# Two half-width matmuls side by side for a last block of 64, a reordered start, and paired row blocks in a two-product SiLU kernel

## The chip, the cores and the metric

One core of a Trainium2 chip. The metric is the device time of one execution in microseconds (us); lower is better.

## The reference, cut to what matters

```python
B, S, D, F = 1, 2048, 640, 1728          # bfloat16
h   = jax.nn.silu(jnp.einsum("bsd,df->bsf", x, w1))
out = jnp.einsum("bsf,fd->bsd", h, w2)
```

The number to notice is F = 1728 = 13 x 128 + 64. The kernel hands the tensor engine blocks of 128 rows by 128 columns (`128*128` in the profile lines below), so F gives 13 full blocks and one block of 64.

## The kernel before

x is transposed to `xT_sb`: chunk 0 (512 rows) on the tensor engine against an identity matrix, the other three chunks by transposing DMAs. The first product computes h transposed, in units of one f-block by 512 rows: five matmuls of 512 columns, one for each 128 rows of D. The matmuls write their sums to `ps1` and `ps2`, the kernel's two tensors in the memory called PSUM. The scalar engine computes the sigmoid from PSUM and the vector engine multiplies it with PSUM into `hT_sb`. The second product runs over 16 row blocks `st` of 128 rows. For each of the FT = 14 f-blocks it issues one matmul of 512 output columns and one of 128 (`DA` and `DB`, together D = 640).

The last f-block is padded with zeros from 64 to 128 and treated like the others:

```python
FT = (F + P - 1) // P                     # 14
N_WARM_MM = 11
...
for i, (sc, ft, c0, n) in enumerate(units):          # first product, ft runs over all 14
    ...
    for dt in range(DT):
        ins = pe.matmul(ps1[:, buf, 0:n],
            lhsT=w1_sb[:, dt, ft * P:(ft + 1) * P],
            rhs=xT_sb[:, dt, col0:col0 + n], start=(dt == 0), stop=(dt == DT - 1))
    ins.then_inc(sem_pe1, 1)
    if i == TP_INSERT_AFTER:                          # 0: after the very first unit
        for j in range(hj, JB):                       # x blocks 2 and 3
            transpose_block(j)
...
for ft in range(FT):                                  # second product
    for (st, ci, b2, c0, ncol) in seg:
        ins = pe.matmul(ps2[:, b2, c0:c0 + ncol],
            lhsT=hT_sb[:, ft, st * P:(st + 1) * P],
            rhs=w2_sb[:, ft, d0:d0 + ncol], start=(ft == 0), stop=(ft == FT - 1))
```

The first two f-blocks of chunk 0 are split into "half-units" of 256 rows, so that work can start when half of this chunk is transposed. Before that, 11 warm-up matmuls on zeros run while x is loaded.

## Time and profile before

The time was 133.96 us (median of 4) when the prediction was made.

| part of the profiled execution (132.13 us) | length |
|---|---|
| head: start to the end of the half-units | 10.26 us |
| first product, 512-column units | 58.27 us |
| second product | 61.02 us |
| end of the last matmul to the end of the span | 2.58 us |

The span runs from the first to the last instruction of the profiled execution; device times are about 1.8 us longer. The borders are starts of matmuls read from the trace; where such a record is missing, as that of the first 512-column matmul here, its start is taken from its neighbours. The last border is the end of the last matmul, and ends of matmuls are modelled by the profiler.

From the page of the kernel before, first the busy time of each engine, then the chain of work that ended last (followed back from the last instruction, at each step to what released it), as shares of the span by engine and by line:

```profile
PE 126.5 (96%) x755; PEld 65.4 (49%) x769; DVE 52.0 (39%) x78; ACT 40.5 (31%) x79; POOL 1.9 (1%) x10
PE 95%; DVE 2%; issue 1%; ACT 0%; POOL 0%; DVEq 0%; POOLq 0%
PE ps L335 46%; PE ps L295 45%; PE ps L246 3%; DVE xT_sb L414 2%; PE ps L260 0%; ACT o_sb L396 0%; POOL z_sb L159 0%; DVEq L413 0%; POOLq L464 0%
```

Line 295 is the first product, line 335 the second, line 246 the warm-up, line 260 the transposes. The chain is tensor engine nearly from end to end. The busy share alone would not say so, because the recorded times of successive matmuls overlap. The groups, kept apart by shape, show this (count, busy us, mean ns of one):

```profile
L335 PE MATMUL ps<-w_sb,hT_sb 128*128 128x512 bf16 x216 | 58.1, 379 | 0.0
L295 PE MATMUL ps<-xT_sb,w_sb 128*128 128x512 bf16 x264 | 58.0, 379 | 0.3
L335 PE MATMUL ps<-w_sb,hT_sb 128*128 128x128 bf16 x224 | 44.6, 219 | 0.4
```

A 512-column matmul is recorded at 379 ns, but its successor starts 216 ns after it; for 128 columns it is 219 ns and 56 ns. What a matmul costs in a dense stream is the distance between starts. The next answer of the profile gives the busy time of each engine in three stretches: 512-column units of the first product, second product, tail.

```profile
core 0: us, PE busy (x) PEld busy (x) DVE busy (x) ACT busy (x) POOL busy (x), PEclk, DMA share, GB/s
10.26:68.53 58.27, 57.95 (x266) 26.41 (x270) 37.07 (x55) 32.07 (x55) 0.00 (x0) 1.00 0.34 79
68.53:129.55 61.02, 60.60 (x441) 34.41 (x447) 12.05 (x17) 4.33 (x15) 0.00 (x0) 1.00 0.11 39
```

The tensor engine fills both stretches; vector and scalar engine have time to spare. (Some matmul records are missing from a trace: there are 270 weight loads but 266 matmuls in the first line.)

The head, as the tensor engine's own timeline (start, length of the merged run, line, shape, count, and the idle time before it with what ended it):

```profile
1.10 4.46 PE L246 MATMUL ps<-z_sb 128*128 128x512 bf16 x11 [1.10 <-POOL z_sb L159]
5.40 0.72 PE L260 MATMUL ps<-ident,x_sb 128*128 128x128 bf16 x10
7.04 0.72 PE L295 MATMUL ps<-xT_sb,w_sb 128*128 128x256 bf16 x5 [0.91 <-DVE xT_sb L414]
7.59 0.72 PE L260 MATMUL ps<-ident,x_sb 128*128 128x128 bf16 x10
8.15 0.71 PE L295 MATMUL ps<-xT_sb,w_sb 128*128 128x256 bf16 x5
9.15 1.27 PE L295 MATMUL ps<-xT_sb,w_sb 128*128 128x256 bf16 x10 [0.29 <-DVE xT_sb L414]
```

Twice the tensor engine stands still, for 0.91 and 0.29 us, until the vector engine's casts (copies with a change of type) of the transposed x are done (line 414).

### The profile page before, as it was taken

How to read it: one execution, taken by the hardware profiler on the slowest of the kernel's cores; microseconds unless marked ns; L12 is line 12 of the kernel's file. 1: busy time of each engine (PE TensorE's matmuls, PEld its weight loads, DVE VectorE, ACT ScalarE, POOL GpSimd, SP SyncE). 2: the span in 40 equal slices, each digit the busy share in tenths (PEclk: the TensorE clock that was granted, in tenths of full speed). 3: DMA queues.
4: the chain of work that ended last, by engine and by line, in shares of the span. 5: the costliest groups of instructions: out<-in, count | busy, mean ns of one | idle time of the engine just before them, and what ended most of it. 6: DMA issues, size and time to landing. Idle time of an engine off the chain costs nothing.

```text
span 132.1 us, 1876 instructions
## 1 busy us (share of the span) xinstructions
PE 126.5 (96%) x755; PEld 65.4 (49%) x769; DVE 52.0 (39%) x78; ACT 40.5 (31%) x79; POOL 1.9 (1%) x10
## 2 busy tenths in 40 slices
PE   6879999999999999999999999999999999999992
PEld 2365444444444444444445555555555555555461
DVE  0164666666666666666662122222102222220121
ACT  4235555555555555555550000000000000000001
POOL 5000000000000000000000000000000000000000
DMA  3897474599800000000000111101111110011103
GB/s 102 249 371 213 100 76 111 100 369 289 159 2 0 5 0 2 0 0 0 0 0 5 50 50 50 40 15 50 50 50 50 54 50 19 31 50 55 50 0 99
DMA packets 15672, 9.78 MB, mean 74 GB/s; under 512 B 8816, under 2 KB 15664, under 8 KB 15664
## 3 DMA queue, kind: packets, MB, share of 16 engines
q1 hardware_dynamic: 14464, 8.95, 25.0%
q10 hardware_dynamic: 1200, 0.72, 1.8%
q8 instruction: 6, 0.10, 0.3%
q14 instruction: 2, 0.02, 0.0%
HBM read 5.08 MB, written 2.62 MB: 58 GB/s over the span
## 4 chain that ended last, share of the span: by engine, by line
PE 95%; DVE 2%; issue 1%; ACT 0%; POOL 0%; DVEq 0%; POOLq 0%
PE ps L335 46%; PE ps L295 45%; PE ps L246 3%; DVE xT_sb L414 2%; PE ps L260 0%; ACT o_sb L396 0%; POOL z_sb L159 0%; DVEq L413 0%; POOLq L464 0%
## 5 line engine op out<-in xcount | busy, mean ns | idle before, releaser
L295 PE MATMUL ps<-xT_sb,w_sb 128*128 128x512 bf16 (+1 forms) x284 | 60.7, 372 | 1.5 <-DVE xT_sb L414 1.2
L335 PE MATMUL ps<-w_sb,hT_sb 128*128 128x512 bf16 (+1 forms) x440 | 60.6, 298 | 0.4
L335 PEld LDWEIGHTS ps<-w_sb,hT_sb 128*128 128x128 bf16 x448 | 34.5, 98 | 26.7
L422 DVE TENSOR_TENSOR hT_sb<-ps,sig_sb 128x512 bf16<-128x512 f32 (+1 forms) x58 | 39.0, 673 | 22.0 <-ACT sig_sb L372 21.9
L295 PEld LDWEIGHTS ps<-xT_sb,w_sb 128*128 128x128 bf16 x290 | 28.2, 98 | 33.5 <-DVE xT_sb L414 1.7
L372 ACT ACTIVATE sig_sb<-ps 128x512 bf16<-128x512 f32 (+1 forms) x58 | 33.7, 583 | 27.0 <-PE ps L295 27.0
L435 DVE CAST o_sb<-ps 128x512 bf16<-128x512 f32 x14 | 9.7, 692 | 42.9 <-PE ps L335 42.9
L384 ACT CAST o_sb<-ps 128x128 bf16<-128x128 f32 x14 | 3.7, 266 | 49.2 <-PE ps L335 49.2
L246 PE MATMUL ps<-z_sb 128*128 128x512 bf16 x11 | 4.5, 590 | 1.1 <-POOL z_sb L159 1.1
L414 DVE CAST xT_sb<-ps 128x384 bf16<-128x384 f32 x4 | 2.0, 553 | 6.1 <-PE ps L260 6.1
L447 DVE CAST o_sb<-ps 128x1024 bf16<-128x1024 f32 x1 | 1.2, 1225 | 5.4 <-PE ps L335 5.4
L246 PEld LDWEIGHTS ps<-z_sb 128*128 128x128 bf16 x11 | 1.5, 144 | 3.6 <-issue 2.5
L396 ACT CAST o_sb<-ps 128x256 bf16<-128x256 f32 x1 | 0.4, 373 | 7.3 <-PE ps L335 7.3
L363 ACT CAST xT_sb<-ps 128x256 bf16<-128x256 f32 x4 | 1.3, 373 | 4.1 <-PE ps L260 4.1
L357 ACT ACT_TABLE_LOAD x1 | 1.3, 1283 | 1.8 <-issue 1.8
L260 PE MATMUL ps<-ident,x_sb 128*128 128x128 bf16 x20 | 1.4, 219 | 0.0
L260 PEld LDWEIGHTS ps<-ident,x_sb 128*128 128x128 bf16 x20 | 1.3, 98 | 0.3
L175 POOL MEMSET w_sb<- 128x640 bf16 x1 | 0.6, 633 | 0.0
L409 DVE MEMSET z_sb<- 128x128 uint32 x1 | 0.2, 165 | 0.8 <-PEq L464 0.8
L172 POOL MEMSET w_sb<- 128x320 bf16 x1 | 0.4, 366 | 0.0
L159 POOL MEMSET z_sb<- 128x256 bf16 x1 | 0.3, 313 | 0.3 <-POOLq L464 0.3
L162 POOL TENSOR_SCALAR_AFFINE_SELECT ident<-ident 128x128 bf16<-128x128 bf16 x1 | 0.3, 294 | 0.2 <-POOL ident L160 0.2
(7 smaller groups left out, 1.0 us busy)
## 6 DMA issues: line engine op xcount, KB each, us to landing
out_dram<-o_sb SPq DMA_DIRECT2D x14, 160.0 KB, 1.8
w_sb<-in_w_dram SPq DMA_DIRECT2D x1, 1120.0 KB, 8.9
w_sb<-in_w_dram SPq DMA_DIRECT2D x1, 960.0 KB, 6.2
w_sb<-in_w_dram SPq DMA_DIRECT2D x1, 880.0 KB, 6.7
w_sb<-in_w_dram SPq DMA_DIRECT2D x1, 640.0 KB, 5.0
x_sb<-in_x_dram SPq DMA_DIRECT2D x1, 320.0 KB, 3.7
x_sb<-in_x_dram ACTq DMA_DIRECT2D x1, 320.0 KB, 4.1
w_sb<-in_w_dram ACTq DMA_DIRECT2D x1, 320.0 KB, 4.6
```

Source lines behind the costliest of these rows:

```text
L246: pe.matmul(ps1[:, NB1 - 1, :], lhsT=z_sb[:, 0:P], rhs=z_sb[:, :], start=True, stop=True,)
L260: ins = pe.matmul(tp_views[wv][:, sl, :], lhsT=x0_sb[:, j, dt * P:(dt + 1) * P], rhs=ident[:, :], start=True, stop=True,)
L295: ins = pe.matmul(ps1[:, buf, 0:n], lhsT=w1_sb[:, dt, ft * P:(ft + 1) * P], rhs=xT_sb[:, dt, col0:col0 + n], start=(dt == 0), stop=(dt == ...
L335: ins = pe.matmul(ps2[:, b2, c0:c0 + ncol], lhsT=hT_sb[:, ft, st * P:(st + 1) * P], rhs=w2_sb[:, ft, d0:d0 + ncol], start=(ft == 0), stop= ...
L357: act.activation(out=warm_sb[:, :], in_=warm_sb[:, :], func=ACT.Sigmoid)
L363: act.copy(out=xT_sb[:, TPV:DT, j * P:(j + 1) * P], in_=tp_views[wv][:, s0_:s0_ + (DT - TPV), :],).then_inc(sem_tpc_a, 1)
L372: act.activation(out=sig_sb[:, buf, 0:n], in_=ps1[:, buf, 0:n], func=ACT.Sigmoid,).then_inc(sem_act1, 1)
L384: act.copy(out=o_sb[:, ob, DA:D], in_=ps2[:, b2, c0:c0 + ncol]).then_inc(sem_ev_a, 1)
L414: dve.tensor_copy(out=xT_sb[:, 0:TPV, j * P:(j + 1) * P], in_=tp_views[wv][:, s0_:s0_ + TPV, :],).then_inc(sem_tpc_v, 1)
L422: dve.tensor_tensor(out=hT_sb[:, ft, col0:col0 + n], in0=ps1[:, buf, 0:n], in1=sig_sb[:, buf, 0:n], op=ALU.mult,).then_inc(sem_dve1, 1)
L435: dve.tensor_copy(out=o_sb[:, ob, 0:DA], in_=ps2[:, b2, c0:c0 + ncol]).then_inc(sem_ev_v, 1)
L447: dve.tensor_copy(out=o_sb[:, obA:obA + 2, 0:DA], in_=ps2[:, bA_, 0:2 * DA].rearrange("p (t c) -> p t c", t=2),).then_inc(sem_ev_v, 1)
```

## The change

The intent is to stop paying a full block for the block of 64. The array is used as two halves. In the first product, the 64 columns of w1 are loaded into column half 0 for one chunk and column half 1 for another, and the two matmuls write PSUM partitions 0 to 63 and 64 to 127. In the second product the 64 rows of h's last block lie in partitions 0 to 63 for even chunks and 64 to 127 for odd ones, so a row block of an even and one of an odd chunk form a pair and use the two row halves. The second product is reordered into eight such pairs, which use `ps1` and `ps2` in turn. The short matmuls ("tail") come last in even pairs and first in odd ones, so that two tails are always neighbours.

With it come a new head (9 warm-up matmuls, all transposes before the first unit) and a new end (the last row block's 512-column part is finished and copied out under its 128-column part). The diff, cut to its core:

```diff
-    N_WARM_MM = 11
+    N_WARM_MM = 9
+            if sc == 3 and ft == 3:
+                units.append((-1, 0, 1, 0))        # tails of chunks 0 and 1
+                units.append((-1, 2, 3, 0))        # tails of chunks 2 and 3
...
-            hj = JB // 2
-            for j in range(hj):
+            for j in range(JB):
                 transpose_block(j)
...
+                    for dt in range(DT):
+                        for hh, scc in enumerate(chs):
+                            ins = pe.matmul(
+                                ps1[hh * 64:hh * 64 + F_LAST, buf, :],
+                                lhsT=w1_sb[:, dt, f0:f0 + F_LAST],
+                                rhs=xT_sb[:, dt, scc * SCH:(scc + 1) * SCH], ...)
...
+                tail_first = p % 2 == 1
+                def tail():
+                    for d0, ncol in ((0, DA), (DA, DB)):
+                        for h, st in enumerate(pr):
+                            ins = pe.matmul(
+                                view[:, h, d0:d0 + ncol],
+                                lhsT=hT_sb[64 * h:64 * h + 64, FT - 1, st * P:(st + 1) * P],
+                                rhs=w2_sb[64 * h:64 * h + 64, FT - 1, d0:d0 + ncol],
+                                start=tail_first, stop=not tail_first, ...)
+                def full(h, st, cols):
+                    for ft in range(FT - 1):
+                        for d0, ncol in cols:
+                            ins = pe.matmul(view[:, h, d0:d0 + ncol], ...)
+                if tail_first:
+                    tail()
+                for h, st in enumerate(pr):
+                    if p == NPAIR - 1 and h == 1:
+                        full(h, st, [(0, DA)])
+                        full(h, st, [(DA, DB)])
+                    else:
+                        full(h, st, [(0, DA), (DA, DB)])
+                if not tail_first:
+                    tail()
```

Cut: memsets, the second copy of w2's last block, semaphore counts, the copies out.

More of the change, by code (lines that the diff above doesn't have):

```diff
@@ L55, in bass_standalone__dense_activation_silu__prompt_kernel, with unit_chunks, tail_half @@
         units.append((0, ft, 0, HN))
-    TP_INSERT_AFTER = 0
     for ft in range(N_SPLIT_FT):
         units.append((0, ft, HN, HN))
-    for ft in range(N_SPLIT_FT, FT):
+    PACK_TAIL = (F_LAST <= 64) and (FT >= 2)
+    FT_REG = FT - 1 if PACK_TAIL else FT
+    for ft in range(N_SPLIT_FT, FT_REG):
         units.append((0, ft, 0, SCH))
     for sc in range(1, NSC):
-        for ft in range(FT):
+        for ft in range(FT_REG):
             units.append((sc, ft, 0, SCH))
-    NU = len(units)
-    chunk_done_cnt = {}
-    for i, (sc, ft, c0, n) in enumerate(units):
-        chunk_done_cnt[sc] = i + 1
+            if sc == 3 and ft == 3:
+                units.append((-1, 0, 1, 0))
+                units.append((-1, 2, 3, 0))
+    if PACK_TAIL and NSC % 2 == 1:
+        units.append((-1, NSC - 1, None, 0))
+    NU = len(units)
+    def unit_chunks(u):
+        if u[0] == -1:
+            return [c for c in (u[1], u[2]) if c is not None]
+        return [u[0]]
+    dve_incs = [len(unit_chunks(u)) if u[0] == -1 else 1 for u in units]
+    dve_val = []
+    acc = 0
+    for inc in dve_incs:
+        acc += inc
+        dve_val.append(acc)
+    chunk_done_cnt = {}
+    for i, u in enumerate(units):
+        for c in unit_chunks(u):
+            chunk_done_cnt[c] = dve_val[i]
+    def tail_half(sc):
+        if not PACK_TAIL:
+            return 0
+        if NSC % 2 == 1 and sc == NSC - 1:
+            return 0
+        return sc % 2
     n_w2_full = FT - 1 if F_LAST != P else FT
     w2_half = n_w2_full // 2
-    n_w2_dmas = 3 if n_w2_full != FT else 2
-    N_INIT = 4 if FP != F else 3
-    N_WARM_MM = 11
+    n_w2_dmas = (4 if (F - (FT - 1) * P) <= 64 else 3) if n_w2_full != FT else 2
+    N_INIT = 3 + (1 if (not PACK_TAIL and FP != F) else 0)
+    N_PAD = 1 if (PACK_TAIL or FP != F) else 0
+    N_WARM_MM = 9
     TPV = 3
@@ L133, in bass_standalone__dense_activation_silu__prompt_kernel, with pe2_need @@
         w2_full_v = w2[0:n_w2_full * P, :].rearrange("(ft p) d -> p ft d", p=P)
-        segs = []
-        for st in range(ST - 2):
-            b2 = st % 2
-            segs.append([(st, 0, b2, 0, DA), (st, 1, b2, DA, DB)])
-        sA, sB = ST - 2, ST - 1
-        segs.append([(sA, 0, 0, 0, DA), (sB, 0, 0, 512, DA)])
-        segs.append([(sA, 1, 1, 0, DB), (sB, 1, 1, 512, DB)])
-        grp_order = []
-        for seg in segs:
-            for g in seg:
-                grp_order.append((g[0], g[1]))
-        grp_idx = {g: i + 1 for i, g in enumerate(grp_order)}
-        seg_done_idx = {}
-        for seg in segs:
-            last = max(grp_idx[(g[0], g[1])] for g in seg)
-            for g in seg:
-                seg_done_idx[(g[0], g[1])] = last
-        grp_loc = {}
-        for seg in segs:
-            for (st, ci, b2, c0, ncol) in seg:
-                grp_loc[(st, ci)] = (b2, c0, ncol)
+        assert PACK_TAIL and NSC == 4 and F_LAST == 64
+        pairs = [(8 * k + q, 8 * k + 4 + q) for k in range(2) for q in range(4)]
+        NPAIR = len(pairs)
+        seq = [st for pr in pairs for st in pr]
+        psv = [
+            ps2[:, :, :],
+            ps1[:, :, :].rearrange("p (t a) s -> p t (a s)", t=2),
+        ]
+        def pe2_need(n, ci):
+            p, h = n // 2, n % 2
+            if p % 2 == 0:
+                return 4 * p + 4
+            if p == NPAIR - 1 and h == 1 and ci == 0:
+                return 4 * p + 3
+            return 4 * p + 2 * h + 2
         @block.gpsimd
@@ L170, in _ @@
             ).then_inc(sem_init, 1)
-            if FP != F:
+            pool.memset(warm_sb[:, :], 0.0).then_inc(sem_init, 1)
+            if PACK_TAIL:
+                pool.memset(hT_sb[:, FT - 1, :], 0.0).then_inc(sem_w2pad, 1)
+            elif FP != F:
                 pool.memset(w1_sb[:, :, F:FP], 0.0).then_inc(sem_init, 1)
-            pool.memset(warm_sb[:, :], 0.0).then_inc(sem_init, 1)
-            if FP != F:
                 pool.memset(w2_sb[:, FT - 1, :], 0.0).then_inc(sem_w2pad, 1)
-            else:
-                pool.memset(warm_sb[:, 0:1], 0.0).then_inc(sem_w2pad, 1)
         @block.sync
@@ L215, in _ @@
                     ).then_inc(sem_w2, 16)
-                    sp.wait_ge(sem_w2pad, 1)
                     if n_w2_full != FT:
-                        sp.dma_start(
-                            out=w2_sb[0:F_LAST, FT - 1, :],
-                            in_=w2[n_w2_full * P:F, :],
-                        ).then_inc(sem_w2, 16)
+                        if PACK_TAIL:
+                            for hh in range(2):
+                                sp.dma_start(
+                                    out=w2_sb[hh * 64:hh * 64 + F_LAST, FT - 1, :],
+                                    in_=w2[n_w2_full * P:F, :],
+                                ).then_inc(sem_w2, 16)
+                        else:
+                            sp.wait_ge(sem_w2pad, N_PAD)
+                            sp.dma_start(
+                                out=w2_sb[0:F_LAST, FT - 1, :],
+                                in_=w2[n_w2_full * P:F, :],
+                            ).then_inc(sem_w2, 16)
             o_cnt = [0] * NOB
-            for st in range(ST - 2):
-                ob = st % NOB
-                sp.wait_ge(sem_ev_v, st + 1)
-                sp.wait_ge(sem_ev_a, st + 1)
+            for n, st in enumerate(seq[:-1]):
+                ob = n % NOB
+                sp.wait_ge(sem_ev_v, n + 1)
+                sp.wait_ge(sem_ev_a, n + 1)
                 sp.dma_start(
@@ L231, in _ @@
                 o_cnt[ob] += 1
-            obA = sA % NOB
-            sp.wait_ge(sem_ev_v, ST - 1)
+            st = seq[-1]
+            ob = (ST - 1) % NOB
+            sp.wait_ge(sem_ev_v, ST)
             sp.dma_start(
-                out=of[sA * P:(sB + 1) * P, 0:DA].rearrange("(t p) c -> p t c", p=P),
-                in_=o_sb[:, obA:obA + 2, 0:DA],
-            ).then_inc(sem_o[obA], 16)
-            o_cnt[obA] += 1
+                out=of[st * P:(st + 1) * P, 0:DA], in_=o_sb[:, ob, 0:DA]
+            ).then_inc(sem_o[ob], 16)
+            o_cnt[ob] += 1
             for ob in range(NOB):
@@ L257, in transpose_block @@
                     pe.wait_ge(sem_x0[j // 2], 16)
+                prev = [jj for jj in range(j) if TP_BANKS[jj % 4] == TP_BANKS[j % 4]]
+                if prev:
+                    pe.wait_ge(sem_tpc_v, max(prev) + 1)
+                    pe.wait_ge(sem_tpc_a, max(prev) + 1)
                 for dt in range(DT):
@@ L275, in _ @@
             tpc_waited = 0
-            for i, (sc, ft, c0, n) in enumerate(units):
+            for i, u in enumerate(units):
                 buf = i % NB1
-                col0 = sc * SCH + c0
-                if sc == 0:
-                    jneed = (c0 + n - 1) // P + 1
-                    if tpc_waited < jneed:
-                        pe.wait_ge(sem_tpc_v, jneed)
-                        pe.wait_ge(sem_tpc_a, jneed)
-                        tpc_waited = jneed
-                elif sc not in x_waited:
-                    pe.wait_ge(sem_x[sc], 16 * DT)
-                    x_waited.add(sc)
+                if u[0] == -1:
+                    chs = unit_chunks(u)
+                    ft = FT - 1
+                else:
+                    sc, ft, c0, n = u
+                    chs = [sc]
+                    col0 = sc * SCH + c0
+                for scc in chs:
+                    if scc == 0:
+                        jneed = JB if u[0] == -1 else (c0 + n - 1) // P + 1
+                        if tpc_waited < jneed:
+                            pe.wait_ge(sem_tpc_v, jneed)
+                            pe.wait_ge(sem_tpc_a, jneed)
+                            tpc_waited = jneed
+                    elif scc not in x_waited:
+                        pe.wait_ge(sem_x[scc], 16 * DT)
+                        x_waited.add(scc)
                 gi = w1_group_of(ft)
@@ L292, in _ @@
                 if i >= NB1:
-                    pe.wait_ge(sem_dve1, i - NB1 + 1)
-                for dt in range(DT):
-                    ins = pe.matmul(
-                        ps1[:, buf, 0:n],
-                        lhsT=w1_sb[:, dt, ft * P:(ft + 1) * P],
-                        rhs=xT_sb[:, dt, col0:col0 + n],
-                        start=(dt == 0),
-                        stop=(dt == DT - 1),
-                    )
-                ins.then_inc(sem_pe1, 1)
-                if i == TP_INSERT_AFTER:
-                    for j in range(hj, JB):
-                        transpose_block(j)
@@ L307, in _ @@
-            pe.wait_ge(sem_w2pad, 1)
+                    pe.wait_ge(sem_dve1, dve_val[i - NB1])
+                if u[0] == -1:
+                    f0 = (FT - 1) * P
+                    for dt in range(DT):
[3 more added lines that the diff above has]
+                                lhsT=w1_sb[:, dt, f0:f0 + F_LAST],
+                                rhs=xT_sb[:, dt, scc * SCH:(scc + 1) * SCH],
+                                start=(dt == 0),
+                                stop=(dt == DT - 1),
+                                skip_group_check=(len(chs) > 1),
+                            )
+                    ins.then_inc(sem_pe1, 1)
+                else:
+                    for dt in range(DT):
+                        ins = pe.matmul(
+                            ps1[:, buf, 0:n],
+                            lhsT=w1_sb[:, dt, ft * P:(ft + 1) * P],
+                            rhs=xT_sb[:, dt, col0:col0 + n],
+                            start=(dt == 0),
+                            stop=(dt == DT - 1),
+                        )
+                    ins.then_inc(sem_pe1, 1)
@@ L308, in _ @@
+            if N_PAD:
+                pe.wait_ge(sem_w2pad, N_PAD)
             pe.wait_ge(sem_w2, 16 * n_w2_dmas)
             dve1_waited = 0
-            ev_waited = 0
-            buf_last_tile = {0: None, 1: None}
-            buf_users = {0: [], 1: []}
-            for seg in segs:
-                need = 0
-                for (st, ci, b2, c0, ncol) in seg:
-                    prev = [t for t in buf_users[b2] if t != st]
-                    if prev:
-                        need = max(need, max(prev) + 1)
-                if need > ev_waited:
-                    pe.wait_ge(sem_ev_v, need)
-                    pe.wait_ge(sem_ev_a, need)
-                    ev_waited = need
-                for (st, ci, b2, c0, ncol) in seg:
-                    if st not in buf_users[b2]:
-                        buf_users[b2].append(st)
-                for (st, ci, b2, c0, ncol) in seg:
-                    sc = (st * P) // SCH
-                    idx_need = chunk_done_cnt[sc]
-                    if dve1_waited < idx_need:
-                        pe.wait_ge(sem_dve1, idx_need)
-                        dve1_waited = idx_need
-                for ft in range(FT):
-                    for (st, ci, b2, c0, ncol) in seg:
-                        d0 = 0 if ci == 0 else DA
-                        ins = pe.matmul(
-                            ps2[:, b2, c0:c0 + ncol],
-                            lhsT=hT_sb[:, ft, st * P:(st + 1) * P],
-                            rhs=w2_sb[:, ft, d0:d0 + ncol],
-                            start=(ft == 0),
-                            stop=(ft == FT - 1),
-                        )
-                        if ft == FT - 1:
-                            ins.then_inc(sem_pe2, 1)
@@ new lines, in need_dve1 @@
+            def need_dve1(v):
+                nonlocal dve1_waited
+                if dve1_waited < v:
+                    pe.wait_ge(sem_dve1, v)
+                    dve1_waited = v
+            for p, pr in enumerate(pairs):
+                view = psv[p % 2]
+                if p == 1:
+                    need_dve1(dve_val[-1])
+                if p >= 2:
+                    pe.wait_ge(sem_ev_v, 2 * (p - 2) + 2)
+                    pe.wait_ge(sem_ev_a, 2 * (p - 2) + 2)
+                for st in pr:
+                    need_dve1(chunk_done_cnt[(st * P) // SCH])
+                tail_first = p % 2 == 1
+                def tail():
+                    for d0, ncol in ((0, DA), (DA, DB)):
+                        for h, st in enumerate(pr):
+                            ins = pe.matmul(
+                                view[:, h, d0:d0 + ncol],
+                                lhsT=hT_sb[64 * h:64 * h + 64, FT - 1, st * P:(st + 1) * P],
+                                rhs=w2_sb[64 * h:64 * h + 64, FT - 1, d0:d0 + ncol],
+                                start=tail_first,
+                                stop=not tail_first,
+                                skip_group_check=True,
+                            )
+                            if not tail_first:
+                                ins.then_inc(sem_pe2, 1)
+                def full(h, st, cols):
+                    for ft in range(FT - 1):
+                        for d0, ncol in cols:
+                            ins = pe.matmul(
+                                view[:, h, d0:d0 + ncol],
+                                lhsT=hT_sb[:, ft, st * P:(st + 1) * P],
+                                rhs=w2_sb[:, ft, d0:d0 + ncol],
+                                start=(ft == 0 and not tail_first),
+                                stop=(ft == FT - 2 and tail_first),
+                                skip_group_check=True,
+                            )
+                            if ft == FT - 2 and tail_first:
+                                ins.then_inc(sem_pe2, 1)
+                if tail_first:
[4 more added lines that the diff above has]
+                        full(h, st, [(DA, DB)])
+                    else:
+                        full(h, st, [(0, DA), (DA, DB)])
+                if not tail_first:
+                    tail()
@@ L366, in _ @@
                 ).then_inc(sem_tpc_a, 1)
-            for i, (sc, ft, c0, n) in enumerate(units):
+            for i, u in enumerate(units):
                 buf = i % NB1
+                n = SCH if u[0] == -1 else u[3]
                 act.wait_ge(sem_pe1, i + 1)
                 if i >= NB1:
-                    act.wait_ge(sem_dve1, i - NB1 + 1)
+                    act.wait_ge(sem_dve1, dve_val[i - NB1])
                 act.activation(
@@ L377, in _ @@
             o_cnt = [0] * NOB
-            for st in range(ST - 2):
-                ob = st % NOB
-                b2, c0, ncol = grp_loc[(st, 1)]
-                act.wait_ge(sem_pe2, seg_done_idx[(st, 1)])
+            for n, st in enumerate(seq):
+                ob = n % NOB
+                act.wait_ge(sem_pe2, pe2_need(n, 1))
                 if o_cnt[ob] > 0:
@@ L384, in _ @@
                 act.copy(
-                    out=o_sb[:, ob, DA:D], in_=ps2[:, b2, c0:c0 + ncol]
+                    out=o_sb[:, ob, DA:D], in_=psv[(n // 2) % 2][:, n % 2, DA:D]
                 ).then_inc(sem_ev_a, 1)
                 o_cnt[ob] += 1
-            obA = sA % NOB
-            bA_, cA_, nA_ = grp_loc[(sA, 1)]
-            bB_, cB_, nB_ = grp_loc[(sB, 1)]
-            assert bA_ == bB_ and nA_ == nB_ == DB and cB_ > cA_
-            act.wait_ge(sem_pe2, seg_done_idx[(sB, 1)])
-            for ob in (obA, obA + 1):
-                if o_cnt[ob] > 0:
-                    act.wait_ge(sem_o[ob], 16 * o_cnt[ob])
-            act.copy(
-                out=o_sb[:, obA:obA + 2, DA:D],
-                in_=ps2[:, bA_, cA_:cA_ + 2 * (cB_ - cA_)].rearrange("p (t c) -> p t c", t=2)[:, :, 0:DB],
-            ).then_inc(sem_ev_a, 1)
-            act.wait_ge(sem_ev_a, ST - 1)
+            st = seq[-1]
+            act.wait_ge(sem_ev_a, ST)
             act.dma_start(
-                out=of[sA * P:(sB + 1) * P, DA:D].rearrange("(t p) c -> p t c", p=P),
-                in_=o_sb[:, obA:obA + 2, DA:D],
+                out=of[st * P:(st + 1) * P, DA:D],
+                in_=o_sb[:, (ST - 1) % NOB, DA:D],
             ).then_inc(sem_ofin, 16)
@@ L417, in _ @@
                 ).then_inc(sem_tpc_v, 1)
-            for i, (sc, ft, c0, n) in enumerate(units):
+            pad_waited = False
+            for i, u in enumerate(units):
                 buf = i % NB1
-                col0 = sc * SCH + c0
                 dve.wait_ge(sem_act1, i + 1)
-                dve.tensor_tensor(
-                    out=hT_sb[:, ft, col0:col0 + n],
-                    in0=ps1[:, buf, 0:n],
-                    in1=sig_sb[:, buf, 0:n],
-                    op=ALU.mult,
-                ).then_inc(sem_dve1, 1)
+                if u[0] == -1:
+                    if not pad_waited and N_PAD:
+                        dve.wait_ge(sem_w2pad, N_PAD)
+                        pad_waited = True
+                    for hh, scc in enumerate(unit_chunks(u)):
+                        dve.tensor_tensor(
+                            out=hT_sb[hh * 64:hh * 64 + F_LAST, FT - 1, scc * SCH:(scc + 1) * SCH],
+                            in0=ps1[hh * 64:hh * 64 + F_LAST, buf, :],
+                            in1=sig_sb[hh * 64:hh * 64 + F_LAST, buf, :],
+                            op=ALU.mult,
+                        ).then_inc(sem_dve1, 1)
+                else:
+                    sc, ft, c0, n = u
+                    col0 = sc * SCH + c0
+                    dve.tensor_tensor(
+                        out=hT_sb[:, ft, col0:col0 + n],
+                        in0=ps1[:, buf, 0:n],
+                        in1=sig_sb[:, buf, 0:n],
+                        op=ALU.mult,
+                    ).then_inc(sem_dve1, 1)
             o_cnt = [0] * NOB
-            for st in range(ST - 2):
-                ob = st % NOB
-                b2, c0, ncol = grp_loc[(st, 0)]
-                dve.wait_ge(sem_pe2, seg_done_idx[(st, 0)])
+            for n, st in enumerate(seq):
+                ob = n % NOB
+                dve.wait_ge(sem_pe2, pe2_need(n, 0))
                 if o_cnt[ob] > 0:
@@ L435, in _ @@
                 dve.tensor_copy(
-                    out=o_sb[:, ob, 0:DA], in_=ps2[:, b2, c0:c0 + ncol]
+                    out=o_sb[:, ob, 0:DA], in_=psv[(n // 2) % 2][:, n % 2, 0:DA]
                 ).then_inc(sem_ev_v, 1)
                 o_cnt[ob] += 1
-            obA = sA % NOB
-            bA_, cA_, nA_ = grp_loc[(sA, 0)]
-            bB_, cB_, nB_ = grp_loc[(sB, 0)]
-            assert bA_ == bB_ and cA_ == 0 and cB_ == DA and nA_ == nB_ == DA
-            dve.wait_ge(sem_pe2, seg_done_idx[(sB, 0)])
-            for ob in (obA, obA + 1):
-                if o_cnt[ob] > 0:
-                    dve.wait_ge(sem_o[ob], 16 * o_cnt[ob])
-            dve.tensor_copy(
-                out=o_sb[:, obA:obA + 2, 0:DA],
-                in_=ps2[:, bA_, 0:2 * DA].rearrange("p (t c) -> p t c", t=2),
-            ).then_inc(sem_ev_v, 1)
 _INS = ['x', 'w1', 'w2']
```

## The prediction

> **What bounds the kernel now.** The tensor engine. The page's busy row gives PE 96% of a 132.1 us span; the chain of waits is 95% PE: the first matrix product (line 295) 45.4%, the second (line 335) 45.7%, warm-up matmuls 3.4%, and casts of transposed x 1.6%. In the chain, first-product matmuls of 512 columns follow each other by about 216 ns; in the second product one f-block (512 + 128 columns) takes about 272 ns. The clock is 1.000. Vector and scalar engines are 39% and 31% busy. Only PE columns, head and tail count.
>
> **What the change does.**
>
> 1. Packing. F = 1728 leaves a last f-block of 64. Before, it costs as much as a full one: 20 matmuls x 216 ns = 4.3 us in product one, 16 x 272 ns = 4.35 us in product two. Now two half-width matmuls share the array (column halves in product one, row halves in product two). If they run together, half goes: 2.16 + 2.17 = 4.3 us. The Trainium skill, "TensorE: Matmul & The Clock Gate", Part 3, reports 2.38x for three column tiles, so I count on real overlap; this trace has no packed matmul to confirm it.
>
> 2. Mode switches. The tails are adjacent: one block in product one, four in product two, so ten switches. The Trainium skill, "TensorEngine Tiling (Array Packing)", Key Properties, says that changing tiling mode drains the engine. Estimate from this trace: a 512-column matmul is recorded at 379 ns but follows its predecessor by 216 ns, so a drain is about 0.16 us; a weight load of 0.10 us may add. Ten switches: 0.7 to 2.6 us, I take 1.4.
>
> 3. Head. Before (timeline): warm-up to 5.56 us, transposes of blocks 0 and 1, a wait for casts to 7.04, half-unit, transposes of blocks 2 and 3, half-unit, wait to 9.15, so full-width units start at about 10.2. Now two warm-up matmuls (0.43 us each) go and all transposes come first (x landed by about 4.8 us). Four vector casts at about 0.51 us spacing from 5.5 end at about 7.5; the half-units run 6.6 to 8.7 without the gap. Full units start at about 8.7: saves 1.5 us. The weights landed in time (group 2 at 9.9 us).
>
> 4. Tail. Before, PE ended at 129.6, then a 0.37 us cast and a 1.7 us output DMA. Now the last cast is 128x128 (0.27 us) and the 512-column part is evicted under the last 13 narrow matmuls: saves 0.2 us.
>
> 5. Off the path: the longer memset of h's last block, one more 80 KB weight load, half-partition multiplies on the vector engine (same count).
>
> Sum: 133.96 - 4.3 + 1.4 - 1.5 - 0.2 = about 129.4 us. Nearly all of it is on the critical path.
>
> **Prediction:** 129.4 us, range 128.2 to 131.2. Faster by over 2%: 0.85; within 2%: 0.14; slower: 0.01.
>
> **What would show each step.** Packed pairs starting within some tens of ns of each other, 0.22 us per pair; ten tail slots of product one in about 2.2 us and a double tail of product two in about 0.55 us plus gaps; gaps of 0.1 to 0.25 us at each switch; first 512-column first-product matmul at about 8.7 us; PE end to span end about 2.3 us instead of 2.5.
>
> **What would make it wrong.** Pairs that serialise (weight loads of one half not hidden under the other), which returns up to 4.3 us and leaves about 133; dearer switches; a clock that is granted later after the shorter warm-up, costing about 1 us; a head that waits for weights instead of x.

## The result

The changed kernel took 128.98 us (median of 11, 128.50 to 129.31) against 134.09 us before (16 executions, 133.26 to 134.58). The ratio is 0.9617, 95% interval 0.9595 to 0.9640: faster. Ratios here are the mean time of one kernel's fast runs over that of the other's of the same rounds, so not quite the ratio of the medians. The predicted 129.4 us was 0.4 us too high.

| part of the profiled execution | before | changed | difference | predicted |
|---|---|---|---|---|
| head to the end of the half-units | 10.26 | 8.33 | -1.93 | -1.5 |
| first product, 512-column units | 58.27 | 56.34 | -1.93 | -2.16 + 2 switches |
| second product | 61.02 | 59.70 | -1.32 | -2.17 + 8 switches |
| last matmul to end of span | 2.58 | 2.32 | -0.26 | -0.2 |
| span | 132.13 | 126.68 | -5.45 | -4.6 |

The page of the changed kernel, busy time and chain:

```profile
PE 122.2 (96%) x752; PEld 62.6 (49%) x767; DVE 51.8 (41%) x79; ACT 39.3 (31%) x78; POOL 2.8 (2%) x9
PE 96%; issue 1%; ACT 1%; POOL 0%; POOLq 0%
PE ps L394 44%; PE ps L346 44%; PE ps L273 3%; PE ps L380 2%; PE ps L335 2%; PE ps L291 1%; ACT xT_sb L434 1%; POOL z_sb L180 0%; ACT o_sb L455 0%; POOLq L525 0%
```

Line 346 is now the first product's full units and line 335 its tails; line 394 is the second product's full matmuls and line 380 its tails. The bottleneck is the same engine at the same share, with less to do. The stretches, cut as before:

```profile
8.32:64.67 56.35, 56.03 (x267) 25.46 (x270) 36.98 (x55) 30.88 (x53) 0.00 (x0) 1.00 0.39 96
64.67:124.37 59.70, 59.12 (x440) 32.86 (x447) 11.82 (x18) 4.19 (x16) 0.00 (x0) 1.00 0.12 42
```

Note that the counts hardly moved: 270 weight loads in the first product before and after, 447 in the second. The change removes no instructions; it lets some of them overlap. The chain in order of time (start, length, what) shows the tail blocks themselves, one in the first product and four in the second:

```profile
52.73 2.28 PE ps L335 x20
71.89 0.65 PE ps L380 x8
86.78 0.65 PE ps L380 x8
101.66 0.65 PE ps L380 x8
116.55 0.65 PE ps L380 x8
```

Twenty matmuls of 512 columns would take 20 x 0.216 = 4.32 us one after the other; here they take 2.28. Starts of matmuls around the first block of the second product, from the trace (program line, columns, ns after the previous start):

```
71676  line 394  128 cols  +216
71828  line 380  512 cols  +152   <- 56 would be normal: 96 ns for the switch
71831  line 380  512 cols    +3   <- the other row half
72055  line 380  128 cols  +224
72058  line 380  128 cols    +3
72110  line 380  512 cols   +52
72114  line 380  512 cols    +4
72326  line 380  128 cols  +212
72330  line 380  128 cols    +4
72478  line 394  512 cols  +148   <- 92 ns for the switch back
```

Pairs start 3 to 4 ns apart. The Trainium skill, "TensorE: Matmul & The Clock Gate", Part 3 (Measured speedup vs the span model), gives about 4 ns for each further tile; this trace agrees. Each change of mode, from the whole array to halves or back, costs some 0.09 us of standstill, plus about 0.01 us in the spacing that follows. The weight loads show a second thing:

```profile
71.82 0.11 PEld L380 LDWEIGHTS ps<-w_sb,hT_sb 64*128 64x128 bf16 x4 [0.26 <-issue]
```

The first weight load of the block starts only 4 ns before its matmul (71824 against 71828), where in the stream before a load starts with the matmul ahead of its own (71462 for the matmul at 71676, whose predecessor starts at 71460). Whether the 0.09 us is the array emptying or the early weight load that is lost, the runs do not tell.

The head after the change:

```profile
1.10 3.56 PE L273 MATMUL ps<-z_sb 128*128 128x512 bf16 x9 [1.10 <-POOL z_sb L180]
4.50 1.00 PE L291 MATMUL ps<-ident,x_sb 128*128 128x128 bf16 x15
5.67 0.45 PE L291 MATMUL ps<-ident,x_sb 128*128 128x128 bf16 x5 [0.17 <-ACT xT_sb L434]
6.13 2.36 PE L346 MATMUL ps<-xT_sb,w_sb 128*128 128x256 bf16 x20
```

The 20 half-unit matmuls now run without a break. And the end, the copies out of PSUM of the kernel before and then of the changed one (instructions of vector and scalar engine and the last output DMAs):

```profile
128.02 1.23 DVE L447 CAST o_sb<-ps 128x1024 bf16<-128x1024 f32 x1 [5.35 <-PE ps L335]
129.59 0.37 ACT L396 CAST o_sb<-ps 128x256 bf16<-128x256 f32 x1 [7.34 <-PE ps L335]
129.99 0.39 ACTq L401 DMA_DIRECT2D out_dram<-o_sb  x1
```

```profile
123.68 0.69 DVE L508 CAST o_sb<-ps 128x512 bf16<-128x512 f32 x1 [2.12 <-remote]
124.40 0.27 ACT L455 CAST o_sb<-ps 128x128 bf16<-128x128 f32 x1 [3.27 <-PE ps L394]
124.70 0.36 ACTq L461 DMA_DIRECT2D out_dram<-o_sb  x1
```

The last cast is 0.10 us shorter; the rest of the 0.26 us lies after it, where the last output transfer is of 32 KB in place of 64 KB.

### The profile page after: what moved, and what is told of

Read it like the earlier page. It is cut to its first block, busy times and chain, and to the rows that moved or that the text cites. A ratio compares the mean times of both kernels' runs of the same rounds, so it can differ in the third digit from the quotient of the medians.

```text
span 126.7 us, 1867 instructions
## 1 busy us (share of the span) xinstructions
PE 122.2 (96%) x752; PEld 62.6 (49%) x767; DVE 51.8 (41%) x79; ACT 39.3 (31%) x78; POOL 2.8 (2%) x9
## 4 chain that ended last, share of the span: by engine, by line
PE 96%; issue 1%; ACT 1%; POOL 0%; POOLq 0%
PE ps L394 44%; PE ps L346 44%; PE ps L273 3%; PE ps L380 2%; PE ps L335 2%; PE ps L291 1%; ACT xT_sb L434 1%; POOL z_sb L180 0%; ACT o_sb L455 0%; POOLq L525 0%
## 5 line engine op out<-in xcount | busy, mean ns | idle before, releaser
L394 PE MATMUL ps<-w_sb,hT_sb 128*128 128x128 bf16 (+1 forms) x407 | 56.7, 297 | 0.6 <-issue 0.2
L346 PE MATMUL ps<-xT_sb,w_sb 128*128 128x512 bf16 (+1 forms) x264 | 56.2, 371 | 0.3
L394 PEld LDWEIGHTS ps<-w_sb,hT_sb 128*128 128x128 bf16 x416 | 31.9, 98 | 25.4 <-issue 1.1
L496 DVE TENSOR_TENSOR hT_sb<-ps,sig_sb 128x512 bf16<-128x512 f32 (+1 forms) x54 | 36.2, 672 | 19.6 <-ACT sig_sb L444 19.2
L346 PEld LDWEIGHTS ps<-xT_sb,w_sb 128*128 128x128 bf16 x270 | 26.3, 98 | 29.8 <-issue 0.4
L444 ACT ACTIVATE sig_sb<-ps 128x512 bf16<-128x512 f32 (+1 forms) x56 | 32.6, 582 | 26.3 <-PE ps L346 25.3
L487 DVE TENSOR_TENSOR hT_sb<-ps,sig_sb 64x512 bf16<-64x512 f32 x4 | 2.8, 689 | 0.6 <-ACT sig_sb L444 0.5
L380 PE MATMUL ps<-w_sb,hT_sb 64*128 64x512 bf16 (+1 forms) x32 | 2.9, 299 | 0.0
L335 PE MATMUL ps<-xT_sb,w_sb 128*64 128x512 bf16 x20 | 2.3, 381 | 0.0
L194 POOL MEMSET hT_sb<- 128x2048 bf16 x1 | 1.8, 1805 | 0.0
```

What stands on the lines that cost most here:

```text
L335: ins = pe.matmul(ps1[hh * 64:hh * 64 + F_LAST, buf, :], lhsT=w1_sb[:, dt, f0:f0 + F_LAST], rhs=xT_sb[:, dt, scc * SCH:(scc + 1) * SCH], s ...
L346: ins = pe.matmul(ps1[:, buf, 0:n], lhsT=w1_sb[:, dt, ft * P:(ft + 1) * P], rhs=xT_sb[:, dt, col0:col0 + n], start=(dt == 0), stop=(dt == ...
L380: ins = pe.matmul(view[:, h, d0:d0 + ncol], lhsT=hT_sb[64 * h:64 * h + 64, FT - 1, st * P:(st + 1) * P], rhs=w2_sb[64 * h:64 * h + 64, FT ...
L394: ins = pe.matmul(view[:, h, d0:d0 + ncol], lhsT=hT_sb[:, ft, st * P:(st + 1) * P], rhs=w2_sb[:, ft, d0:d0 + ncol], start=(ft == 0 and not ...
L444: act.activation(out=sig_sb[:, buf, 0:n], in_=ps1[:, buf, 0:n], func=ACT.Sigmoid,).then_inc(sem_act1, 1)
L487: dve.tensor_tensor(out=hT_sb[hh * 64:hh * 64 + F_LAST, FT - 1, scc * SCH:(scc + 1) * SCH], in0=ps1[hh * 64:hh * 64 + F_LAST, buf, :], in1 ...
```

## The experiments

The theory: (1) halves of the array work at the same time, which is worth 2.16 us in each product; (2) each mode switch costs about 0.1 us, ten of them 1.1 us; (3) the head is worth 1.5 to 1.95 us and the end 0.2 us; (4) these add up, because all lie on the tensor engine's chain. The rivals: a 64-row or 64-column matmul is cheap by itself; the new order of the second product brings the gain; a switch costs nothing, or much more; the early start is lost again later.

All runs are variants of the changed kernel unless stated. In the table, "product one" and "product two" are lengths as in the table above, from the starts of matmuls in each run's trace; the head differs between executions of one kernel (see the head runs).

| run | median us | ratio to before | product one | product two |
|---|---|---|---|---|
| changed kernel | 128.98 | 0.9617 | 56.34 | 59.70 |
| same_rows (wrong) | 131.41 | 0.9796 | 56.35 | 61.85 |
| same_cols (wrong) | 131.29 | 0.9776 | 58.50 | 59.69 |
| split_order | 128.81 | 0.9605 | 56.34 | 59.71 |
| col_order | 129.17 | 0.9636 | 56.59 | 59.70 |
| seven_blocks | 129.83 | 0.9676 | 56.34 | 60.33 |
| unpacked | 132.21 | 0.9868 | 58.27 | 61.02 |
| before_new_head (kernel before) | 132.54 | 0.9887 | 58.27 | 61.02 |
| old_head | 130.84 | 0.9756 | 56.35 | 59.70 |
| warm11 | 129.58 | 0.9672 | 56.35 | 59.69 |
| warm8 | 128.75 | 0.9607 | 56.34 | 59.70 |
| early_x | 128.48 | 0.9584 | 56.35 | 59.70 |
| early_x_bal | 128.43 | 0.9583 | 56.35 | 59.69 |

The lengths of the two products repeat from run to run to about 0.01 us, much better than whole times do. So an edit within a product is judged by its stretch.

### same_rows: both tails of a pair on one row half

```diff
-   lhsT=hT_sb[64 * h:64 * h + 64, FT - 1, st * P:(st + 1) * P],
-   rhs=w2_sb[64 * h:64 * h + 64, FT - 1, d0:d0 + ncol],
+   lhsT=hT_sb[0:64, FT - 1, st * P:(st + 1) * P],
+   rhs=w2_sb[0:64, FT - 1, d0:d0 + ncol],
```

> The changed kernel, but both tail matmuls of a pair in the second product use the same row half (0 to 63), so the result is wrong on purpose for every second row block. Number and shape of matmuls, order, waits and mode switches stay. Theory (two halves of the array run together): the pairs serialise, 8 pairs x 0.272 us = +2.2 us over the changed kernel, about 131.1 us, and the second start of a pair comes 0.216 us after the first in place of 0.003. Rival (a 64-row matmul is cheap by itself, or the gain comes from the new order of the second product): no change, about 129.0 us.

The result was wrong. The second product grew by 2.16 us. One block in this run's chain:

```profile
72.26 1.19 PE ps L380 x8
```

It is 1.19 us in place of 0.65, for the same eight matmuls with the same shapes. A 64-row matmul is not cheap by itself; the gain is the overlap of two halves.

### same_cols: both tails of a unit on one column half

```diff
-   ps1[hh * 64:hh * 64 + F_LAST, buf, :],
+   ps1[0:F_LAST, buf, :],
```

> The changed kernel, but both halves of the first product's tail units write PSUM partitions 0 to 63, so they use the same column half; wrong on purpose. Theory (column halves run together): 10 pairs serialise, 10 x 0.216 = +2.2 us over the changed kernel, about 131.1 us. Rival (a 64-column matmul is cheap by itself): about 129.0 us.

The result was wrong, and the first product grew by 2.16 us. The block in this run's chain:

```profile
53.32 4.43 PE ps L335 x20
```

That is 4.43 us in place of 2.28. Column halves behave like row halves.

### seven_blocks: tails last in pairs 0 to 6

```diff
-   tail_first = p % 2 == 1
+   tail_first = p == NPAIR - 1
```

(and the matching counts for the copies out)

> The changed kernel with the tails of pairs 0 to 6 all last and only pair 7's first: seven tail blocks in the second product in place of four, so six more mode switches and the same matmuls. Theory (about 0.10 us a switch, as the changed kernel's trace shows at 71.7 and 72.4 us): +0.6 us, about 129.6 us. Rival 1 (the prediction's upper estimate, 0.26 us a switch): +1.6 us, about 130.5 us. Rival 2 (no cost of a switch, the 0.85 us came from elsewhere): 129.0 us.

The second product grew by 0.63 us for six more switches, 0.105 us each; the median moved by 0.85 us, part of which is the head of these executions. In the chain, a block of one pair takes 0.38 us where half a block of two takes 0.33:

```profile
72.61 0.38 PE ps L380 x4
80.15 0.38 PE ps L380 x4
...
117.89 0.65 PE ps L380 x8
```

The cost per switch explains what was missing from the ideal 4.33 us in the changed kernel: 0.23 us in the first product (two switches) and 0.85 us in the second (eight). Putting two tails side by side is therefore worth its trouble: six switches here.

### split_order: order A0 B0 A1 B1 in place of A0 A1 B0 B1

```diff
-   for d0, ncol in ((0, DA), (DA, DB)):
-       for h, st in enumerate(pr):
+   for h, st in enumerate(pr):
+       for d0, ncol in ((0, DA), (DA, DB)):
```

> The changed kernel with the four tail matmuls of a pair in the order A0 B0 A1 B1 in place of A0 A1 B0 B1 (A is 512 columns, B 128, the digit is the row half); right result. Theory (matmuls start in program order, so only neighbours of different halves overlap): B0 waits for A0, A1 starts with B0, the pair takes 0.216 + 0.216 + 0.056 = 0.488 us in place of 0.272; 8 x 0.216 = +1.7 us, about 130.7 us. Rival (the two halves are independent streams, order doesn't matter): about 129.0 us.

This expectation failed. The second product took 59.71 us against 59.70, and the blocks still 0.65 us. The built program does have the order 512, 128, 512, 128; the starts in the trace of this run do not:

```
72250  line 380  512 cols
72257  line 380  512 cols    +7
72477  line 380  128 cols  +220
72484  line 380  128 cols    +7
```

The same in this run's timeline of the tensor engine, all that was under way between 72.22 and 72.40 us:

```profile
71.88 0.43 PE L394 MATMUL ps<-w_sb,hT_sb 128*128 128x512 bf16 x2
72.25 0.39 PE L380 MATMUL ps<-w_sb,hT_sb 64*128 64x512 bf16 x2
```

Two 512-column matmuls run and no 128-column one, although the program has one between them. A matmul of row half 1 has passed an earlier one of row half 0. The time agrees: the 1.7 us that strict program order was expected to cost did not appear.

### col_order: five matmuls of column half 0, then five of half 1

```diff
-   for dt in range(DT):
-       for hh, scc in enumerate(chs):
+   for hh, scc in enumerate(chs):
+       for dt in range(DT):
```

> The changed kernel with each tail unit of the first product in the program order: five matmuls of column half 0, then five of half 1 (in place of alternating); right result. The run split_order cost nothing against the theory's +1.7 us, so a matmul of one row half seems to start ahead of an earlier one of the other half. Theory now (halves are fed as separate streams and a later matmul can pass earlier ones of the other half, here by five matmuls and their weight loads): no change, about 129.0 us, starts in pairs 3 to 10 ns apart. Rival (strict program order; split_order was free for another reason, or column halves differ from row halves, or the reach is shorter than five): the halves overlap little, +1.1 us (half 1 of unit one over half 0 of unit two) to +2.2 us, about 130.1 to 131.1 us.

Nearly as the new theory has it, not quite. The first product grew by 0.24 us, the block from 2.28 to 2.52 us:

```profile
53.34 2.52 PE ps L335 x20
```

The starts in the trace are 53265, 53505, 53511, 53721, 53751 and so on. The first matmul of the block runs alone; the second and third start 6 ns apart, and from there two streams run side by side. The unit's last matmul, which carries the semaphore increment, starts at 54398, so in the unit of half 0 starting at 53265, half 1 starts at 53511 and has passed three matmuls of half 0. Which record belongs to which half is inferred from the spacing of 0.216 us within a half; the trace does not name the half. The built program has the written order here too (five of half 0, then five of half 1), so it was not the compiler that mixed them. Strict program order (+1.1 us at least, by the expectation) is excluded. Why half 1 did not pass half 0's second matmul (start 53505) as well stays open.

### unpacked: the new order and head without packing

```diff
-   PACK_TAIL = (F_LAST <= 64) and (FT >= 2)
+   PACK_TAIL = False
```

(tails removed, the full loop over all 14 blocks, pads set to zero as before)

> The changed kernel with head, pairs, PSUM ring and tail as changed, but without packing: the last block of 64 is zero-padded and run as a full block in both products, as in the kernel before. Theory (packing gives 4.3 us less about 1.05 us of switches): +3.3 us over the changed kernel, about 132.3 us. Rival (the new order and ring of the second product bring a part of the gain by themselves): nearer 131 us, with the rest of the difference to before larger than head and tail explain.

The two products took 58.27 and 61.02 us, equal to the kernel before to the hundredth. The pairs and the turns between `ps1` and `ps2` bring nothing and cost nothing by themselves. The gap from the last matmul to the end was 2.27 us, so the end's gain (0.31 us here, 0.26 us in the changed kernel) does not depend on packing.

### before_new_head, old_head, warm11: the head

before_new_head is the kernel before with 9 warm-up matmuls and all transposes first; old_head is the changed kernel with the old head; warm11 is the changed kernel with 11 warm-up matmuls alone.

```diff
# old_head, against the changed kernel
-    N_WARM_MM = 9
+    N_WARM_MM = 11
-            for j in range(JB):
+            for j in range(JB // 2):
                 transpose_block(j)
...
+                if i == 0:
+                    for j in range(JB // 2, JB):
+                        transpose_block(j)
```

> The kernel before with only the new head: 9 warm-up matmuls and all transposes before the first unit. Theory (head and packing add up, head worth 1.5 to 1.95 us): about 132.3 us. Rival (the later phases absorb an earlier start, for instance in waits for weights or x): about 134 us.

> The changed kernel with the old head: 11 warm-up matmuls and transposes 2 and 3 after the first unit. Theory: +1.5 to +1.95 us, about 130.7 us. Rival (only the number of warm-up matmuls matters): the same as the run warm11.

> The changed kernel with 11 warm-up matmuls in place of 9, transposes in the new order. Theory (part of the head's gain is the two warm-up matmuls, 0.43 us each at half clock or 0.22 at full; the rest is the order): +0.4 to +0.9 us, about 129.6 us, less than old_head by 0.8 to 1.2 us. Rival (order alone): no change, 129.0 us. Rival (warm-ups alone): equal to old_head, about 130.7 us.

The new head on the old kernel brought 1.4 us (132.54 against 133.91 in the same rounds; by the interval of the ratio, 1.1 to 2.0 us). The old head on the changed kernel cost 1.9 us and the two warm-up matmuls alone 0.6 us (130.84 and 129.58 against 128.98, which is from other rounds). The four runs of warm11 lie between 128.75 and 130.04 us and its interval (0.9617 to 0.9727) overlaps that of the changed kernel, so the share of the warm-ups is likely rather than settled. The order of the transposes counts: the waits of 0.91 and 0.29 us for casts, 0.66 and 0.29 us in old_head, give way to one of 0.17 us. Nothing later takes the gain back: in before_new_head both products are as long as before.

The head's length differs between executions of one kernel, mostly because the tensor engine is not at full rate from the start, and the moment at which it gets there moves. In three profiles, from the tensor engine's timeline: the changed kernel, seven_blocks (same head), old_head:

```profile
4.50 1.00 PE L291 MATMUL ps<-ident,x_sb 128*128 128x128 bf16 x15
```

```profile
4.91 1.92 PE L291 MATMUL ps<-ident,x_sb 128*128 128x128 bf16 x20
6.84 2.36 PE L346 MATMUL ps<-xT_sb,w_sb 128*128 128x256 bf16 x20
```

```profile
5.77 1.27 PE L291 MATMUL ps<-ident,x_sb 128*128 128x128 bf16 x10
7.70 0.72 PE L346 MATMUL ps<-xT_sb,w_sb 128*128 128x256 bf16 x5 [0.66 <-DVE xT_sb L477]
```

Warm-up matmuls start 0.427 us apart and, once the clock is full, 0.216. In the profile of the changed kernel this happens from the start at 4.06 us on, in that of before between 4.92 and 5.19, in seven_blocks not before the last warm-up, in old_head not in any of its 11. (The clock column of the profile does not show this: it reads 1.00 between 1 and 3 us as well. The spacing does.) The Trainium skill, "TensorE: Matmul & The Clock Gate", Part 1, says that the window which decides this is free-running and does not reset when a kernel starts; the scatter here agrees, though no run shows the window itself. In one of the profiles, same_rows, x was the limit instead: its chain begins with the load of x, which ends at 4.73 us, and the first transpose follows at 4.87 us although the clock was full by then. The half-units ended at 10.26 and 10.92 us in the two profiles of the old head and at 8.33 to 9.04 us in eight of the new one (mean 8.82), a mean difference of 1.8 us. The profiled execution of the changed kernel had its clock early and was among its fastest (128.50 us).

### warm8, early_x, early_x_bal: towards a better version

The head runs show that the ninth warm-up often ends after x has landed. warm8 drops it. early_x loads x of blocks 0 and 1 by transfers of their own and has 7 warm-ups. early_x_bal in addition moves one of the five 128-column slices that are cast in each x block from the vector to the scalar engine.

```diff
# early_x_bal, against the changed kernel (early_x is the same with TPV = 3)
-    N_WARM_MM = 9
-    TPV = 3
+    N_WARM_MM = 7
+    TPV = 2
# first queue
-   out=x0_sb[:, 0:hj, :], in_=x0_v[:, 0:hj, :]
+   out=x0_sb[:, 0:1, :], in_=x0_v[:, 0:1, :]
+   ...then: out=x0_sb[:, hj:JB, :], in_=x0_v[:, hj:JB, :]
# second queue
-   out=x0_sb[:, hj:JB, :], in_=x0_v[:, hj:JB, :]
+   out=x0_sb[:, 1:hj, :], in_=x0_v[:, 1:hj, :]
```

> The changed kernel with 8 warm-up matmuls in place of 9. In most profiles of the new head the clock is still at half rate when the ninth warm-up ends, and the first transpose starts at 4.91 us while x has landed by 4.4 us. Theory (the head waits for the warm-ups in most executions): first transpose at about 4.5 us, up to -0.4 us, about 128.7 us. Rival (fewer warm-ups let the clock come later, or x is the limit): 129.0 us or more.

> An attempt at a better head: x of block 0 and of block 1 are loaded by transfers of their own (one on each queue), blocks 2 and 3 after them, 7 warm-up matmuls. If x bounds the head, the first transpose comes at about 4.1 us (end of the seven warm-ups at half clock), casts about 0.5 us earlier, the first unit at about 6.0 us: -0.3 to -0.6 us against the changed kernel, about 128.5 us. Rival (w1's first group, landed at about 5.8 us, or the clock bounds it): within 0.2 us of 129.0.

> The run early_x with the casts of transposed x divided 2 to 3 between vector and scalar engine in place of 3 to 2 (0.55 us a block on the vector engine before, estimated 0.42 and 0.48 us now). If the casts bound the head: up to 0.3 us less than early_x, about 128.3 us. Rival: the same as early_x.

The medians were 128.75, 128.48 and 128.43 us, ratios 0.9607, 0.9584 and 0.9583. All three results were correct. For warm8 the 0.2 us are within the noise; in its profile the first transpose, at 4.63 us, has waited 0.17 us for x, so dropping warm-ups alone soon meets the load of x. The tensor engine's head in the profile of early_x_bal:

```profile
1.10 3.17 PE L276 MATMUL ps<-z_sb 128*128 128x512 bf16 x7 [1.10 <-POOL z_sb L180]
4.06 1.79 PE L294 MATMUL ps<-ident,x_sb 128*128 128x128 bf16 x20
5.75 3.21 PE L349 MATMUL ps<-xT_sb,w_sb 128*128 128x256 bf16 x24
```

Transposes start at 4.06 us. Against the changed kernel early_x and early_x_bal save about 0.5 us in 129, early_x_bal with executions of 128.12 to 128.71 against 128.50 to 129.31; the two were timed in different rounds, each against the kernel before, and their intervals overlap (0.9546 to 0.9621 and 0.9595 to 0.9640). So a small gain is likely rather than settled. Whether the other division of the casts adds anything can't be read from 0.05 us. In the profile of early_x a new wait of 0.19 us for w1 appears at 8.36 us (the weight load's; the matmul starts some 0.08 us late). w1's later groups are now issued at 5.06 us in place of 4.37, which probably is the reason: the next limit of this head.

## Why the prediction was right, point by point

- **Bound.** Right. The tensor engine's chain was the time before and after (95% and 96%), and unpacked shows that reordering alone moves nothing.
- **Packing, -4.3 us.** Right in mechanism and size. Undoing the overlap gave back 2.16 us (same_rows) and 2.16 us (same_cols).
- **Mode switches, +1.4 us.** Right in kind, somewhat too large: 1.08 us, 0.105 us a switch. The 1.4 was picked from a range of 0.7 to 2.6 us, so that it came within 0.3 us is partly luck. The estimate took a drain of 0.16 us from the difference of recorded length and spacing of a matmul; the measured standstill is 0.09 us. The Trainium skill, "TensorEngine Tiling (Array Packing)", Key Properties, says that changing the mode drains the engine; the runs agree with a cost at each change.
- **Head, -1.5 us.** Right in kind, too small in the profile: -1.93 there, -1.8 as a mean over the profiles, between -1.4 and -1.9 in whole times. The prediction had half-units from 6.6 to 8.7 us; the profile had 6.13 to 8.33, other profiles of the same head start them at 6.5 to 6.8, and the mean end of all eight is 8.82. So the predicted times were good for this head in general, and the profiled execution was an early one. The prediction named a later clock after the shorter warm-up as a risk, but not that the moment of the full clock moves between executions of one kernel.
- **End, -0.2 us.** Measured -0.26.
- **Total.** 129.4 predicted, 128.98 measured. Switches and head, about 0.3 us each in the same direction, more than cover the difference of 0.4 us; the base of the sum, 133.96 us, was itself 0.13 us below the later median. The sizes did not come out right by errors that cancel.
- **What would show it wrong.** Pairs did not serialise, switches were not dearer, the head did not wait for w1. A later clock after the shorter warm-up is not seen: by the spacing of starts the latest moment is in old_head, with 11 warm-ups; a handful of profiles does not settle it.

One belief, written down in the expectation of split_order and not in the prediction, was wrong without harm: that matmuls of different halves start in program order. split_order refutes it.

## What to carry to other kernels

A remainder of 64 in a blocked dimension need not cost a full block: two matmuls on different halves of the array take the time of one (here 2.28 us in place of 4.43 for twenty), for about 0.1 us at each change of mode, so collect them in few blocks (here five blocks, 1.1 us, against 4.3 us gained). Judge such a change by the distance between starts of matmuls and by the length of the stretch concerned, not by busy shares or matmul counts, which stayed the same here. In a kernel bound by one engine from end to end, the head is worth the same look: 1.4 to 1.9 of the 5.1 us came from the order of the first few instructions and two warm-up matmuls fewer.

## What the Trainium skill lacked or had wrong

- "TensorE: Matmul & The Clock Gate", Part 2 (step 1) says that matmuls stay in program order and Part 3 (The mechanism) that they are strictly first in, first out. In these runs a matmul of the other half starts before an earlier one: split_order issues 512, 128, 512, 128 columns and the trace has 512, 512 (7 ns later), 128 (220 ns later), 128, at no cost in time (59.71 against 59.70 us); in col_order one half passes three matmuls of the other and the block takes 2.52 us in place of 2.28. The page's advice that one increment on the last matmul covers all of a pack rests on that order, so it should be checked where the halves are not issued in step. No run here showed a wrong result from it.
- "TensorEngine Tiling (Array Packing)", Key Properties, says that a change of mode drains the engine, without a size. Here a change costs 0.105 us (six more changes of row halves, +0.63 us); the standstill is alike for row halves (96 and 92 ns) and column halves (94 and 95 ns).
- "TensorE: Matmul & The Clock Gate", Part 3, has its measured speedups for three tiles and more. For two halves in a dense stream the runs show 4.43 us against 2.28 us for 20 column-half matmuls, 1.94 times, two switches included in both.
